# A new instruction order for attention, 480 slots per expert, and a third expert's weights loaded before the experts begin

## The chip, the cores and the metric

The kernel runs on one core of one Trainium2 chip. The metric is the device time of one launch in microseconds (us); lower is better.

## The reference

Attention with normalized queries and keys is followed by a mixture of experts in which a hash of the token's number chooses the one expert that a token goes to. All tensors are float32 and the token ids int64.

```python
batch, n_heads, seq, head_dim = (8, 12, 448, 64)
N, D, E, F = (3584, 768, 8, 1024)

def rmsnorm(x, g):
    rms = np.sqrt(np.mean(x * x, axis=-1, keepdims=True) + 1e-06)
    return x / rms * g
q_n, k_n = (rmsnorm(q, g_q), rmsnorm(k, g_k))
scores = scale * np.matmul(q_n, k_n.transpose(0, 1, 3, 2))     # scale = 1 / sqrt(64)
attn = softmax(scores)                                          # max taken off, sum + 1e-9
attn_out = np.matmul(attn, v)

x = attn_out.transpose(0, 2, 1, 3).reshape(B * S, H * D)        # one row per token
expert_idx = token_ids * 2654435761 % E
for e in range(E):
    mask = expert_idx == e
    h = np.maximum(x[mask] @ w1[e], 0.0)                        # w1[e]: 768 x 1024
    out[mask] = h @ w2[e]                                       # w2[e]: 1024 x 768
```

The inputs are the same draw each time.

## The kernel before

**Attention.** An image (one entry of the batch) has 12 heads, worked on as 6 pairs. One pair is one step, so there are 48 steps. Steps are put together in groups whose normalization is prepared at once: image 0 is cut into groups of 1, 2 and 3 pairs, every other image into two groups of 3, which makes 17 groups. The raw q, k and v of two images share one buffer each, and there are two buffers of each kind; GpSimd's queue loads them, with a cast to float16 or bfloat16. The pair 0 of image 0 comes in float32 through SyncE's and ScalarE's queues.

A group is prepared by squares of q and k (`prep_sq`, L275 on VectorE or L273 on ScalarE), sums of squares over the head dimension by matmuls with the identity (`prep_sum`, L287), their last reduction (`prep_red`, L298), logarithm and exponential on ScalarE for the inverse root (`prep_rr`, L306 and L307), the products (`prep_norm`, L319), and a copy of v beside a column of ones (`prep_v`, L330).

A step transposes its normalized q and k on PE (L477) into one PSUM bank of the pool `ps_qk`, which has one buffer and also takes the sums of squares. VectorE copies the bank out as kT and qT (L487, L489). Four pieces of scores (`score`, L498 and L503) go to three buffers of `ps_sc`; ScalarE takes their exponentials (L500, L505). `av_part` (L522 to L534) multiplies them with v in three parts; the ones give the row sums. VectorE then takes the reciprocal (L542) and the product (L543). When the 6 pairs of an image are done, its rows are stored to a scratch tensor in memory (`store_x`).

The order is written out by hand: every engine executes its instructions in program order, and within a step the program emits pieces 1 and 2 of the scores, the next step's transposes, piece 3, the former step's AV parts, the next step's piece 0 and what the lists `pre`, `mid` and `post` say is due. From step 14 on each step also emits one of 26 side jobs (`p1` to `p11`, `table`, `table_mm`) that turn token ids into slots and a table of row numbers per slot, `gidx`.

**Slots.** Each expert has CAP = 512 slots, 4 tiles of 128. The first three tiles of an expert hold only tokens of images 0 to 6, so that they can be gathered before image 7 is stored. Tokens that don't fit go to overflow blocks, worked through in a loop at the end with a count `n_ov` that is computed on the chip.

**Experts.** GpSimd gathers rows of the scratch tensor by `gidx` (L173), PE transposes them (`put_xT`, L184), `gemm1` multiplies with w1 over up to 512 columns of slots (L766), ScalarE and VectorE apply the maximum with zero (L770, L772), `gemm2` multiplies each tile of slots with w2 (L779), the result is copied out (L783) and scattered to the output rows (L784). Weights lie in four buffers: `w_pool` has two (experts 0, 1, 4, 5) and `w_pool2` two (experts 2, 3, 6, 7). Those of experts 0 and 1 are loaded during attention (L156, L162), those of 2 to 7 during the expert stage in six pieces each (`w_pieces`, `w_next`, L830), with expert e + 4's asked for when expert e is done. `fetch(e + 2)` asks for gathers two experts ahead. `turn(e + 1, kt)` transposes one tile of the next expert ahead of each tile of GEMM 2. The gathers of expert 0's first three tiles are emitted at step 44, and their transposes (to `xT_e`) after the last score piece.

All loads of q, k, v and weights, the gathers and the scatters are issued by GpSimd in its program order. Each of them waits until the transfer eight before it has landed, because eight semaphores are used in turn.

Of the kernel before, what the change touches and what calls it, by code (L numbers as in the profile page):

```python
# [19 lines left out]
def kernel(  # L20
# [28 lines left out]
    CAP = 512  # L49
    KT = CAP // P  # L50
# [26 lines left out]
    xg_e = [m_xe.tile([P, DIN], FP16, name=f"xg_{t}") for t in range(KT - 1)]  # L77
    xT_e = m_xe.tile([P, CO, CAP], FP16, name="xT_e")

# [24 lines left out]
    def setup():  # L104
        import dataclasses as _dc
        tid_t32 = _dc.replace(moe_token_ids.tensor, shape=[N * 2], dtype=I32)
        for base in (0, D):
            nc.sync.dma_start(out=gcol[base:base + D, 0:1], in_=g_q[:, None])
            nc.sync.dma_start(out=gcol[base:base + D, 1:2], in_=g_k[:, None])
        nc.scalar.dma_start(out=tid32[:],  # L110
                            in_=bass.AP(tensor=tid_t32, offset=0,
                                        ap=[[2 * NTC, P], [2, NTC], [1, 2]]))
# [36 lines left out]
    def load_w1(e, pool, dyn=None):  # L149
        w1_sb = pool.tile([P, CO, F], FP16, name="w1_sb")  # L150
# [8 lines left out]
    def load_w2(e, pool, dyn=None):  # L159
        w2_sb = pool.tile([P, FO, DIN], FP16, name="w2_sb")  # L160
# [4 lines left out]
    def load_w(e, pool):  # L165
        w_tiles[e] = (load_w1(e, pool), load_w2(e, pool))
# [32 lines left out]
    with tc.manual_schedule(), \  # L199
# [15 lines left out]
        q_bufs = [a_nat.tile([P, 2 * HP, 8, D], FP16, name=f"qr_{t}") for t in range(NB)]  # L215
        k_bufs = [a_nat.tile([P, 2 * HP, 8, D], FP16, name=f"kr_{t}") for t in range(NB)]
# [49 lines left out]
        def prep_sq(gi, a, on_act=False):  # L266
# [5 lines left out]
            if on_act:  # L272
# [4 lines left out]
        def prep_sum(gi, a, wide=False):  # L277
# [3 lines left out]
            if wide:  # L281
                T = ps_sc.tile([P, 2, 512], FP32, name="sc_ps")[:, 0]
            else:
                T = ps_qk.tile([P, 512], FP32, name="qkT_ps")
# [14 lines left out]


        def prep_rr(gi):
            n = groups[gi][2]
            ss = st[gi].pop("ss")
            m = 8 * n
            rr = a_st.tile([P, 2, GMAX * 8, 2], FP16, name="rr")
            nc.scalar.activation(ss[:, :, 0:m], ss[:, :, 0:m], AF.Ln, bias=eps_col[:], scale=1.0 / D)  # L306
# [3 lines left out]
            st[gi]["n8"] = a_n8.tile([P, 2, GMAX, 4, 2, D], FP16, name="n8")  # L310

        def prep_norm(gi):
            n = groups[gi][2]
            rr = st[gi].pop("rr")
            n8 = st[gi]["n8"]
            for a in (1, 0):
                f = raw(a, gi).rearrange("p n (hh j) (u t) -> p n hh j u t", hh=2, t=2)
                for hh in range(2):
                    nc.vector.tensor_tensor(  # L319
                        out=n8[:, a, 0:n, :, hh, :].rearrange("p n j (u t) -> p n j u t", t=2),  # L320
                        in0=f[:, :, hh],
                        in1=rr[:, a, 4 * n * hh:4 * n * hh + 4 * n].rearrange(
                            "p (n j) t -> p n j t", j=4)[:, :, :, None, :].to_broadcast(
                                [P, n, 4, D // 2, 2]),
                        op=ALU.mult)
# [63 lines left out]
        def p4():  # L389
# [6 lines left out]
            V.tensor_scalar(out=t1[:], in0=hole[:], scalar1=float(P - 1 - CAP), scalar2=0.0,  # L396
# [5 lines left out]
        def p5():  # L402
# [4 lines left out]
                            scalar2=float(E * CAP - CAP), op0=ALU.mult, op1=ALU.add)  # L407
# [13 lines left out]
        def p7():  # L421
            V.scalar_tensor_tensor(out=over[:], in0=rank[:], scalar=float(CAP), in1=bc(add_e[:]),
# [42 lines left out]
        qkt = {}  # L465
        pend = {}
        xs = {}

        def transposes(s, evac=True):
            gi, i = steps[s]  # L470
            n8 = st[gi]["n8"]
            T32 = ps_qk.tile([P, 512], FP32, name="qkT_ps")
            T = T32[:].bitcast(FP16)
            for a in (1, 0):
                for j in range(4):
                    o = 512 * a + P * j
                    nc.tensor.transpose(T[:, o:o + P], n8[:, a, i, j].rearrange("p h d -> p (h d)"),  # L477
                                        ident16[:])
            qkt[s] = T
            if evac:  # L480
                transposed(s)

        def transposed(s):
            T = qkt[s]
            kT = a_qk.tile([P, 512], FP16, name="kT")
            qT = a_qk.tile([P, S], FP16, name="qT")
            nc.vector.tensor_scalar(out=kT[:], in0=T[:, 512:1024], scalar1=g_col[:], scalar2=None,  # L487
                                    op0=ALU.mult)
            nc.vector.tensor_copy(qT[:], T[:, 0:S])  # L489
            qkt[s] = (qT, kT)  # L490

        def score(s, j):
            qT, kT = qkt[s]
            expT = pend[s][0]
            sc = ps_sc.tile([P, 2, 512], FP32, name="sc_ps")
            if j < 3:
                for hh in range(2):
                    nc.tensor.matmul(sc[:, hh, :S], lhsT=kT[64 * hh:64 * hh + 64, P * j:P * j + P],  # L498
                                     rhs=qT[64 * hh:64 * hh + 64, :], start=True, stop=True)
                nc.scalar.activation(expT[:, 2 * j:2 * j + 2, :], sc[:, :, :S], AF.Exp,  # L500
                                     bias=0.0, scale=1.0)
            else:
                nc.tensor.matmul(sc[:, 0, :S], lhsT=kT[:, 384:512], rhs=qT[:, :],  # L503
                                 start=True, stop=True)
                nc.scalar.activation(expT[:, 6, :], sc[:, 0, :S], AF.Exp, bias=0.0, scale=1.0)  # L505
                qkt.pop(s)
# [421 lines left out]
```

## Time and profile before

| | us |
|---|---|
| Median of 3 runs (lowest, highest) | 379.61 (378.47, 381.21) |
| The profiled execution | 374.72 |
| Span of that execution, first to last instruction | 373.2 |
| PE busy, share of the span | 343.4, 92% |
| VectorE (DVE) busy | 216.1, 58% |
| ScalarE (ACT) busy | 190.3, 51% |
| GpSimd (POOL) busy | 175.6, 47% |

The profile is of one execution. In its lines L12 is line 12 of the kernel, PEld is the weight load of a matmul, a form such as 128x512 is partitions by elements, and xN counts instructions. A timeline line has the start, the duration, the engine and its line, the operation with output<-input, and in brackets the idle time before it and what ended that. A line of windows has the stretch, its length, then for PE, PEld, DVE, ACT and POOL the busy time and in parentheses the number of instructions, then the granted PE clock as a share of full speed, a measure of DMA use and the GB/s moved. An average over the span says little here, since attention and experts have different limits; the stages have to be read one by one.

### The profile page before, as it was taken

To read this page: it belongs to the slowest core of one execution; us is meant where nothing else is said; L and a number is where in the kernel's file an instruction comes from. 1 tells how busy PE (TensorE), PEld (TensorE's weight loads), DVE (VectorE), ACT (ScalarE), POOL (GpSimd) and SP (SyncE) were. 2 spreads that over 40 slices of the span, in tenths; PEclk is the share of its full clock that TensorE was granted. 3 is DMA by queue.
4 is the path that set the end of the run, shared out by engine and by line. 5 is a ranking of instruction groups with operands and counts; after the bars stand their busy time and mean duration, and the time that the engine had idled before them with its cause. 6 is when DMAs were issued, how large, how long until landed. Compare 5 with 4: busy or idle time off the path is not lost. (4 is left out here: it accounts for less than half of the span.)

```text
span 373.2 us, 9220 instructions
## 1 busy us (share of the span) xinstructions
PE 343.4 (92%) x3862; PEld 231.1 (62%) x3862; DVE 216.1 (58%) x514; ACT 190.3 (51%) x288; POOL 175.6 (47%) x247
## 2 busy tenths in 40 slices
PE   7778879999989999999899999999998997999992
PEld 3456656767666666675676766666665664666661
DVE  4578979999999999989443333232232232332311
ACT  4777879999989999999312121211111111111110
POOL 8887981027439930003328335463654645633122
PEclk9999999999999999999899999999999999999997
DMA  8999999927999992274536999999999999972112
GB/s 123 159 192 195 185 221 191 216 40 127 194 211 211 223 217 52 46 162 108 128 93 141 209 238 252 211 261 223 203 254 177 250 219 188 241 259 91 58 42 112
DMA packets 54268, 64.59 MB, mean 173 GB/s; under 512 B 22403, under 2 KB 42134, under 8 KB 53968
## 3 DMA queue, kind: packets, MB, share of 16 engines
q0 software_dynamic: 50592, 57.98, 88.4%
q1 hardware_dynamic: 3024, 5.41, 5.3%
q8 instruction: 31, 0.51, 0.6%
q10 hardware_dynamic: 608, 0.59, 0.5%
q14 instruction: 13, 0.11, 0.1%
HBM read 89.68 MB, written 18.09 MB: 289 GB/s over the span
## 5 line engine op out<-in xcount | busy, mean ns | idle before, releaser
L500 ACT ACTIVATE expT<-sc_ps 128x896 bf16<-128x896 f32 x144 | 125.2, 923 | 10.8 <-PE sc_ps L498 9.8
L779 PE MATMUL o_ps<-w_sb,h_sb 128*128 128x256 f16 (+1 forms) x512 | 87.9, 326 | 0.0
L766 PEld LDWEIGHTS <-w_sb 128*128 128x128 f16 x432 | 58.0, 144 | 26.4 <-issue 2.0
L766 PE MATMUL h_ps<-xT,w_sb 128*128 128x512 f16 x336 | 73.7, 379 | 0.0
L779 PEld LDWEIGHTS <-h_sb 128*128 128x128 f16 x512 | 48.8, 98 | 32.7
L770 ACT ACTIVATE h_sb<-h_ps 128x512 f16<-128x512 f32 (+2 forms) x36 | 19.7, 549 | 77.2 <-PE h_ps L766 77.2
L784 POOL DMA_INDIRECT out_dram<-o_sb,gidx x32 | 32.9, 1029 | 49.0 <-ACT o_sb L783 17.0
L772 DVE TENSOR_SCALAR h_sb<-h_ps 128x512 f16<-128x512 f32 (+2 forms) x36 | 22.8, 632 | 56.3 <-PE h_ps L766 56.3
L173 POOL DMA_INDIRECT xg<-x_scratch,gidx x32 | 32.5, 1016 | 43.1 <-DVE xg L846 16.0
L783 ACT COPY o_sb<-o_ps 128x768 f32<-128x768 f32 x16 | 12.8, 798 | 74.8 <-PE o_ps L779 56.4
L498 PE MATMUL sc_ps<-qT,kT 64*128 64x448 f16 x288 | 44.0, 356 | 3.7 <-DVE qT L489 2.1
L522 PEld LDWEIGHTS <-expT 128*128 128x128 bf16 x864 | 37.0, 98 | 9.8 <-DVE x_sb L543 6.3
L522 PE MATMUL av_ps<-v,expT 128*128 128x65 bf16 x864 | 40.6, 194 | 1.5 <-DVE x_sb L543 1.5
L783 DVE COPY o_sb<-o_ps 128x768 f32<-128x768 f32 x16 | 15.3, 958 | 43.1 <-PE o_ps L779 21.2
L830 POOL DMA_DIRECT2D w_sb<-in_moe_w_dram x36 | 23.1, 648 | 31.2 <-DMA w_sb<-in_moe_w_dram 29.8
L477 PEld LDWEIGHTS <-n 128*128 128x128 f16 x384 | 22.4, 97 | 24.7 <-issue 15.4
L477 PE MATMUL qkT_ps<-ident,n 128*128 128x128 f16 x384 | 30.3, 220 | 6.7 <-DVE ss L298 3.8
L543 DVE TENSOR_TENSOR x_sb<-av_ps,srec 128x448 f16<-128x448 f32 x48 | 29.7, 619 | 1.5
L185 DVE COPY xT<-xT_ps 128x768 f16<-128x768 f16 x28 | 15.5, 554 | 25.3 <-PE xT_ps L184 25.2
L287 PEld LDWEIGHTS <-ident 128*128 128x128 f16 x544 | 23.6, 98 | 9.1 <-issue 6.5
L505 ACT ACTIVATE expT<-sc_ps 128x448 bf16<-128x448 f32 x48 | 26.9, 560 | 1.1 <-PE sc_ps L503 1.1
L487 DVE TENSOR_SCALAR kT<-qkT_ps,g_col 128x512 f16<-128x512 f16 x48 | 23.0, 480 | 4.1 <-PE qkT_ps L477 3.4
(145 smaller groups left out, 422.6 us busy)
## 6 DMA issues: line engine op xcount, KB each, us to landing
w_sb<-in_moe_w_dram POOLq DMA_DIRECT2D x32, 384.0 KB, 13.1
w_sb<-in_moe_w_dram POOLq DMA_DIRECT2D x12, 768.0 KB, 14.1
x_scratch<-x_sb SPq DMA_DIRECT2D x15, 288.0 KB, 5.9
w_sb<-in_moe_w_dram POOLq DMA_DIRECT2D x2, 1536.0 KB, 14.5
kr<-in_k_dram POOLq DMA_DIRECT2D x6, 384.0 KB, 10.2
qr<-in_q_dram POOLq DMA_DIRECT2D x3, 768.0 KB, 14.5
vr<-in_v_dram POOLq DMA_DIRECT2D x6, 384.0 KB, 19.8
kr<-in_k_dram POOLq DMA_DIRECT2D x6, 288.0 KB, 10.0
```

The lines of the kernel that those rows point to most:

```text
L173: nc.gpsimd.indirect_dma_start(out=xg[:], out_offset=None, in_=x_dram[0:rows, :], in_offset=bass.IndirectOffsetOnAxis(ap=idx, axis=0), bou ...
L287: nc.tensor.matmul(sp.rearrange("p (hh n j) w -> p hh n (j w)", hh=2, j=4), lhsT=ident16[:], rhs=sq[:, c, 0:m].rearrange("p (n hh j) w -> ...
L477: nc.tensor.transpose(T[:, o:o + P], n8[:, a, i, j].rearrange("p h d -> p (h d)"), ident16[:])
L498: nc.tensor.matmul(sc[:, hh, :S], lhsT=kT[64 * hh:64 * hh + 64, P * j:P * j + P], rhs=qT[64 * hh:64 * hh + 64, :], start=True, stop=True)
L500: nc.scalar.activation(expT[:, 2 * j:2 * j + 2, :], sc[:, :, :S], AF.Exp, bias=0.0, scale=1.0)
L505: nc.scalar.activation(expT[:, 6, :], sc[:, 0, :S], AF.Exp, bias=0.0, scale=1.0)
L522: nc.tensor.matmul(av[:, 2 * t + hh, :], lhsT=expT[:, tl(hh, j), P * t:P * t + P], rhs=v8[:, i, 4 * hh + j, 0:D + 1], start=(hh == 0 and t ...
L543: nc.vector.tensor_tensor(out=x_sb[:, :, hp * D:hp * D + D], in0=av[:, :, :D], in1=srec[:, :, None].to_broadcast([P, SL, D]), op=ALU.mult)
L766: nc.tensor.matmul(h_ps[:, :c1 - c0], lhsT=w1v[:, co, fo, :], rhs=xT[:, co, c0:c1], start=(co == 0), stop=(co == CO - 1))
L779: nc.tensor.matmul(o_ps[:, d0:d1], lhsT=h_sb[:, fo, col * P:(col + 1) * P], rhs=w2_sb[:, fo, d0:d1], start=(fo == 0), stop=(fo == FO - 1))
L783: (nc.vector.tensor_copy if col % 2 else nc.scalar.copy)(o_sb[:], o_ps[:])
L784: scat = nc.gpsimd.indirect_dma_start(out=out[:, :], out_offset=bass.IndirectOffsetOnAxis(ap=idx, axis=0), in_=o_sb[:], in_offset=None, bo ...
```

## The change

Three things change.

1. Attention's order. The loops over steps with `pre`, `mid` and `post` are replaced by text lists of tokens. One list covers the opening (steps 0 to 8 and parts of 9), and one block, `steady`, is emitted for each group from 4 on. A token is one operation: `sqq`, `sumk`, `redq`, `nk:1.0` and so on for a group, `Tk`, `kT`, `sc`, `exp`, `av`, `rec`, `x` for a step; numbers are relative to the group or step. For this `prep_norm`, `transposes`, `transposed`, `score` and the end of `av_part` are split into smaller pieces. Squares run on ScalarE for k of group 0 and k of group 3 (before: k and q of group 1, k of group 2).
2. A new prologue. The first loads bring q ahead of k; images 0 and 1 are loaded by half images and 2 to 7 one image at a time, each as q, k, v (before: images 2 and 3, 4 and 5, 6 and 7 together, first all k, then q, then v). GpSimd clears the second buffers before it loads image 2. The gains come in two transfers instead of four.
3. Experts use FIT = 480 of 512 slots, so the last tile of each has 96 (`LAST`). The weights of expert 2 go to the buffers that held raw q and k of images 0, 1, 4 and 5 (`qk_keep`, `w_views`) and their loads are emitted at steps 41 and 42; expert 6 uses the same buffers later. `w_pool2` has one buffer instead of two.

The core of the diff:

```diff
+    FIT = 480
+    LAST = FIT - 3 * P
...
+    qk_keep = [m_xe.tile([P, 2 * HP, 8, D], FP16, name=f"{a}r_0") for a in "qk"]
...
+    def w_views():
+        q0, k0 = [t[:].rearrange("p n s d -> p (n s d)") for t in qk_keep]
+        return (q0.rearrange("p (c f) -> p c f", f=F), k0.rearrange("p (f d) -> p f d", d=DIN))
...
+        ACT_SQ = ((0, 1), (3, 1))
+        WIDE_SUM = ((0, 0), (1, 0), (1, 1))
...
+        load_q([nc.sync, nc.scalar], first[:, 0], 0, 0, 1)
+        load_kv([nc.sync, nc.scalar, nc.sync, nc.scalar], first[:, 1], k, 0, 0, 1)
+        setup()
         nc.vector.memset(warm[:], 0.0)
...
+        load(0, 1, 2, "q")
+        make_identity(nc, ident16[:])
+        load(0, 1, 2, "k")
+        load(0, 0, 3, "v")
+        load(0, 3, 3)
+        load(1, 0, 3)
+        load(1, 3, 3)
         zero_kv(nc.gpsimd, k_bufs[1], 0, 2 * HP)
         zero_q(nc.gpsimd, q_bufs[1], 0, 2 * HP)
         zero_kv(nc.gpsimd, v_bufs[1], 0, 2 * HP)
+        load(2, 0, HP)
+        load(3, 0, HP)
+        for xg in xg_e:
+            nc.gpsimd.memset(xg[:], 0.0)
         setup2()
...
+        def hooks(s):
...
+            if s == HP:
+                load(4, 0, HP)
+            if hp == 3 and 1 <= b and b + 4 < B:
+                load(b + 4, 0, HP)
             if side and s >= 14:
                 side.pop(0)()
...
             if s == NS - 4:
                 for kt in range(KT - 1):
                     gather(xg_e[kt], gidx[:, kt:kt + 1], N_EARLY)
             if hp == 3:
...
                 if b == 6:
+                    w_tiles[1].append(load_w2(1, new_w2(w_pool)))
+            if b == 6 and hp == 5:
+                w_tiles[2] = w_views()
+                load_w1(2, w_tiles[2][0])
+            if b == 7 and hp == 0:
+                load_w2(2, w_tiles[2][1])
...
+        emit("""
+            zero:2 zero:0 zero:4 zero:1 sqq:0 zero:3 spin:9 sumq:0 sqk:0 sumk:0 spin:3 redq:0
+            sqq:1 redk:0 gain:0 ln:0 er:0 sumq:1 spin:1 redq:1 nk:0.0 sqk:1 nk:0.1 sumk:1 spin:1
+            nq:0.0 zero:5 nq:0.1 redk:1 ln:1 Tk:0 Tq:0 kT:0 qT:0 sc:0.0 er:1 sc:0.1 nk:1.0 nk:1.1
+            sc:0.2 nq:1.1 nq:1.0 exp:0.0 Tk:1 kT:1 exp:0.1 Tq:1 v:0 exp:0.2 qT:1 sc:1.0 exp:1.0
+            Tk:2 sc:0.3 sqk:2 Tq:2 av:0.0 kT:2 exp:0.3 qT:2 sc:1.1 sqq:2 sc:1.2 sc:1.3 sumk:2
...
+        """, 0, 0)
+        steady = """
+            Tk:1 Tq:1 sc:0.1 sc:0.2 av:-1.0 kT:1 av:-1.1 qT:1 exp:0.1 exp:0.2 v:1 sc:0.3 sumq:1
+            sqk:2 redq:1 av:-1.2 sc:1.0 sc:1.1 exp:0.3 ln:1 sc:1.2 er:1 Tk:2 exp:1.0 Tq:2 rec:-1
+            x:-1 av:0.0 nk:1.0 kT:2 qT:2 av:0.1 exp:1.1 sc:1.3 av:0.2 sumk:2 sc:2.0 exp:1.2
+            nk:1.1 sc:2.1 exp:1.3 nq:1.0 sc:2.2 exp:2.0 rec:0 nq:1.1 redk:2 Tk:3 x:0 Tq:3 av:1.0
+            kT:3 exp:2.1 av:1.1 qT:3 sqq:2 sc:2.3 av:1.2 rec:1 sc:3.0 exp:2.2 exp:2.3 x:1 exp:3.0
+        """
+        for g in range(4, NG):
+            emit(steady, g, s0[g])
...
-         tc.tile_pool(name="w_pool2", bufs=2) as w_pool2, \
+         tc.tile_pool(name="w_pool2", bufs=1) as w_pool2, \
...
         def gemm2(w2_sb, h_sb, col, idx, free=True):
+            w = LAST if free and col == KT - 1 else P
...
         fetch(1, range(KT - 1))
-        queue += w_pieces(2)
-        w_next(1)
         fetch(0, [KT - 1])
         fetch(1, [KT - 1])
         fetch(2, range(KT))
-        w_next(len(queue))
         queue += w_pieces(3)
...
-                gemm1(w1_sb, xTs.pop(e), h_sb, 0, CAP)
+                gemm1(w1_sb, xTs.pop(e), h_sb, 0, FIT)
...
-                    gemm1(w1_sb, xTs.pop(0), h_sb, EARLY, CAP)
+                    gemm1(w1_sb, xTs.pop(0), h_sb, EARLY, FIT)
```

The thresholds in `p4`, `p5` and `p7` that decide which tokens overflow use FIT in place of CAP; the distance between experts in the slot numbers stays 512. The hooks (loads, side jobs, gathers) of step s are emitted after the product `x` of step s - 1.

## Prediction

> **What bounds the kernel now.** I read the page's slices first, then busy time by stage, then the timelines of PE, DVE and POOL at the three places that the change touches. The chain of waits is no help: it ends after one step at the last scatter.
>
> ```profile
> PE   7778879999989999999899999999998997999992
> ...
> DVE  4578979999999999989443333232232232332311
> ACT  4777879999989999999312121211111111111110
> ...
> DMA  8999999927999992274536999999999999972112
> ```
>
> A slice is 9.3 us. There are two kernels in one: attention up to slice 19 (about 180 us), where DVE, ACT and PE are all near 9, and the experts, where PE alone is full. DMA has holes late in attention (slices 15 to 20) and is full during the experts.
>
> ```profile
> 50.00:55.00 5.00, 4.05 (x74) 2.81 (x73) 2.64 (x7) 3.78 (x5) 4.13 (x6) 1.00 1.37 236
> ...
> 80.00:100.00 20.00, 19.43 (x343) 13.79 (x342) 19.62 (x51) 18.95 (x29) 11.76 (x21) 1.00 0.87 125
> 100.00:120.00 20.00, 18.33 (x323) 12.86 (x319) 19.37 (x52) 18.40 (x29) 12.26 (x18) 1.00 1.50 209
> 120.00:140.00 20.00, 18.92 (x331) 13.20 (x328) 19.80 (x55) 18.64 (x29) 13.75 (x20) 1.00 1.03 219
> ```
>
> In these windows the third engine column is DVE and the fourth ACT. Between 60 and 160 us DVE is busy 97.7 of 100 us: it sets the pace of steady attention, whatever the order. The first 60 us are different: DVE 44.4 us, so 15.6 idle, 2.4 of them in the first row shown.
>
> ```profile
> 156.52 0.63 POOL L162 DMA_DIRECT2D w_sb<-in_moe_w_dram  x1 [22.75 <-PE sc_ps L498]
> 172.79 1.14 POOL L173 DMA_INDIRECT xg<-x_scratch,gidx  x1 [15.65 <-DVE xg L846]
> ...
> 178.47 0.50 PE L184 MATMUL qkT_ps<-ident,xg 128*128 128x128 f16 x6
> ...
> 185.90 2.98 PE L766 MATMUL h_ps<-xT_e,w_sb 128*128 128x384 f16 x17
> ```
>
> The hand-over: POOL issues w2 of expert 1 once the slot table's matmuls are through, and the gathers of expert 0 when image 6 is stored; PE transposes those rows at 178.47 and runs the bulk of the first GEMM from 185.90.
>
> ```profile
> 209.20 10.52 PE L766 MATMUL h_ps<-xT,w_sb 128*128 128x512 f16 x48
> 219.56 0.50 PE L184 MATMUL xT_ps<-ident,xg 128*128 128x128 f16 x6
> ...
> 286.97 0.51 PE L184 MATMUL xT_ps<-ident,xg 128*128 128x128 f16 x6 [0.95 <-DMA xg<-x_scratch,gidx]
> ...
> 296.37 0.50 PE L184 MATMUL xT_ps<-ident,xg 128*128 128x128 f16 x6 [0.41 <-DVE xT L185]
> ...
> 311.71 0.51 PE L184 MATMUL xT_ps<-ident,xg 128*128 128x128 f16 x6 [1.89 <-DMA xg<-x_scratch,gidx]
> ```
>
> In the experts PE is gapless but for these 3.25 us: gathers that landed late.
>
> **The Trainium skill.** "TensorE: Matmul & The Clock Gate", section "Wait — 56ns, not 53.3ns?", puts back-to-back matmuls at N columns over 2.4 GHz plus 2.5 ns. The trace agrees: 48 of 512 columns start over 10.36 us, 215.8 ns each. The same page, "What's actually happening", says that after a mostly idle window of about 3.4 us PE runs at half clock until it was busy as long; here PE is busy 0.35 to 0.76 of each us from 177 to 181, and 181 to 184 shows clocks of 0.54 and 0.50. "DMA: Bandwidth & Descriptors", section "Queues, rings and completion order": each DMA engine takes the descriptors of one queue in order and takes turns between queues. POOL's transfers indeed land in the order of issue throughout this trace, gathers and scatters behind weights, while SP's stores squeeze in between.
>
> **The change, part by part.** The sum is against the profiled execution, 374.72 us with a span of 373.2; the runs shown have a median of 379.61, 4.9 more. I carry the difference over.
>
> *480 slots.* The largest expert needs 465 slots (counted from the given token ids, holes for early slots included), so no overflow block arises. Seven experts x 48 matmuls go from 512 to 480 columns: 336 x 13.3 ns = 4.5 us. Expert 0's late slice goes from 128 to 96 columns; its 48 took 2.89 us, 60.2 ns each; by the page's rule 96 columns take 42.5, by no gain 60.2; I take 13.3 ns less, 0.6 us. GEMM 2 of the last tile streams the same 768 columns of w2, so its 96 slots save nothing on PE. Evacuations get shorter beside PE. Sum 5.1 (4.5 to 5.4).
>
> *Third expert early, as seen from the experts.* POOL's first gather per expert is issued at 223.94, 247.43, 270.57, 295.04, 318.72: 23.7 us apart, while PE needs 22.1 per expert (209.20, 231.30, 253.40, 275.50). DMA is slower than PE there, and PE lives on a lead until 286. Taking out five pieces of expert 2's weights (issued from 200.28, landed 206.2 to 219.4, so about 15 us of queue) gives that back. PE will need 21.5 per expert, so DMA then loses about 2.5 per expert over four experts, 10 us, less than 15. The 3.25 us go. If the lead does not hold, they stay. Experts in all: 5.1 + 3.25 = 8.4 saved (5.1 to 8.7).
>
> *Third expert early, as seen from the hand-over.* POOL does not follow the steps; it stops only at real waits. Right after w2(1) it can issue w1(2) and w2(2), since their buffers (raw q and k of images 4 and 5) were last read before 150. In coordinates of before: w2(1) issued 156.5, landed 167.5 (10.96 us). w1 pieces land 1.86 apart (118.74, 120.66, 122.52, 124.37), four 7.4; a whole w2 behind others took 7.7 (124.37 to 132.03); image 6's stores in between about 1.5 (in a like case a piece needed 3.3 instead of 1.86). So w2(2) lands at 184.1, and expert 0's gathers, behind it on one queue, at 185, 186 and 187, where before they landed at 176.0, 177.3 and 179.7. PE wants the first at 178.5: what waits behind is everything on PE, the last two AV parts and with them image 7's stores. Transposes end about 187.5 instead of 181.3. In the new PE order two of three AV(46) parts are ahead of them, so what follows is 0.3 + 1.0 (six GEMM matmuls) + 1.2 (AV 47) and half clock, 1.75 lost, as before had too: 42 GEMM matmuls start at an equivalent 191.8 against 185.9. Cost 5.9 us. From below: if the queue ran 3 us faster, 2.5; from above, with w2 at the 4.65 us per half that the experts' stage shows, 8.5. I take 5.9.
>
> *Prologue.* Squares of group 0 now run on DVE and ACT side by side (before one after the other on DVE, 0.69 and 0.68), and q comes first. Walked with the trace's durations: sq q 4.5, sums and ss to 7.0, rr 7.65; sq of k of group 1 waits for its keys (issue about 3 to 5 behind q and the identity, some 4 us to land) until 9.0; norms to 10.7; kT and qT to 11.9; first exp 12.3 against 13.69. Then transfers gate: keys of group 2 land about 16.4 (DVE ready at 14.4), of group 4 about 28.4 (27.3). Half-image loads need 40 POOL issues of about 0.65 us, until 27.6, then the zeroing of the second buffers (4.7 us, before behind all loads) comes ahead of image 2, whose keys land near 41.5; DVE is ready about 39. DVE work of the opening list after the first square: evacuations 7.2, row sums and x 6.3, squares 7.3, norms 8.9, v 2.2, sums and gain 2.6: 34.5. With these waits the list ends at about 50.5, having done 39 us of DVE work. Before reached 36.8 at 50 and then lost 2.4 on late values of image 2, which now come with their image. DVE has 0.9 more to do in all (three squares come from ACT, two go; zeros of v). Of 160.1 us, 121.1 remain, at the old share of 0.969 (114.8 of the 118.5 us from 60 to 178.5) until about 175.5 against 178.5; I add 1 us for steady blocks nearer full. Lead 4 us (0 to 9: from no gain, to 15.6 idle with half removed and no key late).
>
> *Steady blocks.* Same instructions, DVE-bound at 9.4 to 10 us per three steps; at most 2.3 us were idle. From 160 ACT is full instead (2.81 us a step), and nothing changes there.
>
> *Nothing:* tokens' load moved to SP (used at 72), gains in two transfers (needed about 7), later POOL constants (needed near 70), reciprocal split from the product. Hidden by the distance; if POOL's constants were late, side work would slip, not steps.
>
> Sum: -4.0 + 5.9 - 8.4 = -6.5. Profiled 368.2, median 379.6 - 6.5 = 373.1.
>
> **Rivals.** *Both covers hold (B):* image 2's keys are in time (lead 9) and the gathers cost only 2.5: -9 + 2.5 - 8.4 = -14.9, 364.7. For it: 15.6 us idle in the opening. Against: DMA is already at 9 in slices 1 to 7. *Order is worth nothing (C):* DVE was the bound, the opening is bound by transfers: 0.5 lead, -0.5 + 5.9 - 8.4 = -3.0, 376.6. For: DMA row; against: the chain to the first exp is plainly shorter. *Slower (D):* one PSUM bank serves all transposes and square sums, and the block of three steps interleaves sums with transposes; where DVE's reduction sits behind norms, PE waits for the bank, then DVE for PE. Before, PE waited up to 1.87 us at L477 on the reduction. A new wait of 0.8 us in each of 13 blocks adds 10.4: -4 + 10.4 + 5.9 - 8.4 = +3.9, 383.5; above 0.5 us per block it outweighs all gains. Against: each reduction stands well ahead of the next transposes in the list.
>
> **How the numbers follow.** Forecast 0.48, B 0.20, C 0.20, D 0.12. 1% (3.8 us) is about what a measurement of this kernel tells from no change. Faster by more: nearly all of the forecast (0.42), B, a little of C (0.04): 0.66. Within: 0.06 + 0.15 + 0.03: 0.24. Slower: 0.10. The range goes from B's time to a new wait of 0.55 us a block (-4 + 7.2 + 5.9 - 8.4 = +0.7): 364.7 to 380.3.
>
> **What would show it.** Right: GEMM 1 blocks of 9.7 us; no DMA wait at the experts' transposes; expert 0's gathers landing right after w2(2), PE idle 5 to 6 us before the first xT_e transposes, then half clock; first exp near 12.3; DVE stopped at image 2's key square near 39 to 42. Wrong: gathers landing before the weights, DVE under 95% between 60 and 160, or experts still waiting for gathers.

## The result, and the profile after

The changed kernel takes 391.75 us (median of 4 runs, 390.35 to 392.46) where the kernel before takes 379.04 on the same chip (4 runs): ratio 1.0325, 95% interval 1.0267 to 1.0383. It is slower by 12.7 us; 6.5 us faster was forecast. Chips differ: in later comparisons the kernel before had medians between 373.1 and 381.3 us, and a second comparison of the changed kernel gave 391.55 against 373.14, ratio 1.0489 (1.0407 to 1.0572). So I compare ratios, or kernels run on one chip. The profiled execution of the changed kernel took 390.35 us, with a span of 388.8, 15.6 more than the one before; that is more than the 12.7 of the medians, because the profiled execution before, with 374.72 us, was faster than the four runs measured beside the changed kernel (377.75 at the lowest).

First the slices of its page, 9.7 us each.

```profile
PE   6789699824999999989929999999999999999992
...
DVE  5689689642999999979713343333223333233310
ACT  3578689903999999979911112111211111121110
...
PEclk9589899955999999999957999999999999999999
DMA  8998998999699883229972399999999999912112
```

There is a hole that the kernel before has not: slices 8 and 9, counted from 0 (78 to 97 us), with ACT down to 0, DVE to 2 and PE's clock to half, while DMA stays at 9. The second weak place, slice 20, is the hand-over, the passage from attention to the experts. Next, the windows of the changed kernel from 60 us on, columns as before (PE, PEld, DVE, ACT, POOL); below them stands the window from 60 to 80 of the kernel before, whose windows from 80 to 140 the prediction shows.

```profile
60.00:80.00 20.00, 16.50 (x306) 12.08 (x305) 14.30 (x35) 17.88 (x28) 12.88 (x22) 0.99 1.21 171
80.00:100.00 20.00, 9.63 (x128) 6.80 (x130) 9.78 (x27) 6.15 (x9) 10.43 (x21) 0.58 1.39 177
100.00:120.00 20.00, 19.56 (x338) 13.46 (x335) 19.27 (x50) 18.91 (x29) 10.63 (x18) 1.00 1.15 171
120.00:140.00 20.00, 18.74 (x330) 13.01 (x328) 19.45 (x56) 18.55 (x29) 18.58 (x25) 1.00 0.87 178
140.00:160.00 20.00, 19.34 (x339) 13.58 (x337) 19.86 (x56) 19.12 (x31) 6.64 (x10) 1.00 0.51 100
```

```profile
60.00:80.00 20.00, 19.15 (x336) 13.62 (x335) 19.34 (x50) 19.12 (x30) 0.43 (x3) 1.00 1.33 169
```

From 100 to 160 DVE is busy 58.6 of 60 us: the steady block itself runs as forecast. From 60 to 100 DVE is busy 24.1 of 40 us, where the kernel before had 39.0. What ended its idle time stands in the timelines at that place: first POOL's, then lines of DVE, PE and ACT, and last the same two operations of the side jobs (POOL and DVE) in the kernel before.

```profile
70.49 0.75 POOL L239 DMA_DIRECT2D qr<-in_q_dram  x1 [0.92 <-DVE kT L496]
...
82.14 0.64 POOL L249 DMA_DIRECT2D vr<-in_v_dram  x1 [0.94 <-DMA qr<-in_q_dram]
82.78 0.22 POOL L377 CAST eidf<-eid 128x28 f32<-128x28 int32 x1
...
92.81 0.64 POOL L249 DMA_DIRECT2D vr<-in_v_dram  x1 [0.87 <-DMA qr<-in_q_dram]
93.45 0.20 POOL L384 CAST oc<-ot 128x8 bf16<-128x8 f32 x1
```

```profile
83.04 0.39 DVE L381 TENSOR_TENSOR onehot<-eidf,iota_f 128x224 bf16<-128x224 f32 x1 [7.85 <-POOL ones_e L378]
93.94 0.39 DVE L395 CAST cmix<-sc_ps 112x224 bf16<-112x224 f32 x1 [6.59 <-PE sc_ps L393]
93.71 0.17 PE L392 MATMUL sc_ps<-oc,emask 128*128 128x8 bf16 x1 [5.31 <-POOL oc L384]
87.05 2.54 ACT L525 ACTIVATE expT<-sc_ps 128x896 bf16<-128x896 f32 x3 [9.10 <-PE sc_ps L507]
```

```profile
72.19 0.21 POOL L367 CAST eidf<-eid 128x28 f32<-128x28 int32 x1 [13.17 <-DVE eid L365]
75.27 0.38 DVE L371 TENSOR_TENSOR onehot<-eidf,iota_f 128x224 bf16<-128x224 f32 x1
```

The conversion of the expert ids (side job p1, L377) takes 0.22 us on POOL, but POOL executes in order and has the ten transfers of image 5 in front of it, from 70.49 to 82.78. VectorE's next side operation (p2, L381) reads its result and waits 7.85 us, with all of VectorE's steady work queued behind it. In the kernel before GpSimd had nothing to do there: it waited 13.17 us for VectorE, converted at once, and VectorE's line has no bracket, so no wait. In the changed kernel the same happens again right away with p2's own conversion (L384), behind image 6: PE waits 5.31 us, VectorE for PE 6.59 us, ScalarE for scores 9.10 and 6.49 us. The transfers themselves were not urgent: image 5's first step is step 30, its keys are squared from step 24 on, and this is step 15. The last piece of exponential of step 16 comes at 77.4 us (76.7 before), that of step 19 at 102.9 (87.0 before).

The hand-over and the experts:

```profile
171.73 0.62 POOL L168 DMA_DIRECT2D w_sb<-in_moe_w_dram  x1 [25.08 <-PE sc_ps L462]
...
174.76 0.59 POOL L168 DMA_DIRECT2D kr<-in_moe_w_dram  x1
...
194.01 1.13 POOL L182 DMA_INDIRECT xg<-x_scratch,gidx  x1 [18.66 <-DVE xg L871]
...
200.71 0.82 PE L193 MATMUL qkT_ps<-ident,xg 128*128 128x128 f16 x6 [6.62 <-DMA xg<-x_scratch,gidx]
...
208.89 7.51 PE L788 MATMUL h_ps<-xT_e,w_sb 128*128 128x384 f16 x42
...
226.62 3.05 PE L788 MATMUL h_ps<-xT_e,w_sb 128*128 128x96 f16 x48 [0.65 <-DVE xT_e L194]
...
232.44 9.88 PE L788 MATMUL h_ps<-xT,w_sb 128*128 128x480 f16 x48
```

GpSimd issues w2 of expert 2 (into `kr`) at 174.76, and 19 us later the gathers, for which image 6 has to be stored first. PE waits 6.62 us for the gathered rows, then runs at half clock (an early transpose group takes 0.82 us instead of 0.50). A GEMM 1 block takes 9.88 instead of 10.52 us. To compare kernels I use three marks of the PE timeline: the 28 matmuls of the slot table (step 39), the bulk of expert 0's first GEMM, and the end of the span, in us:

| kernel | slot table | first GEMM | end | table to GEMM | GEMM to end |
|---|---|---|---|---|---|
| before | 155.09 | 185.90 | 373.2 | 30.8 | 187.3 |
| changed | 170.30 | 208.89 | 388.8 | 38.6 | 179.9 |
| changed, second comparison | 173.69 | 211.78 | 391.2 | 38.1 | 179.4 |
| changed, loads in pairs | 158.42 | 197.12 | 376.2 | 38.7 | 179.1 |
| changed, side jobs on VectorE | 157.03 | 195.74 | 375.2 | 38.7 | 179.5 |
| before, single loads | 159.16 | 188.47 | 375.9 | 29.3 | 187.4 |
| changed, gathers first | 172.23 | 202.97 | 390.2 | 30.7 | 187.2 |
| changed, weights ahead | 171.70 | 200.92 | 380.4 | 29.2 | 179.5 |
| before, experts' part | 157.08 | 196.38 | 375.7 | 39.3 | 179.3 |
| both moves | 158.93 | 188.15 | 367.2 | 29.2 | 179.1 |
| both moves, image 1 whole | 155.24 | 184.46 | 363.4 | 29.2 | 178.9 |
| both moves, more idle matmuls | 160.33 | 191.08 | 370.2 | 30.8 | 179.1 |
| both moves, image 1 whole, more idle matmuls | 154.99 | 184.21 | 363.1 | 29.2 | 178.9 |
| the same, later copy of values | 154.88 | 192.54 | 371.9 | 37.7 | 179.4 |
| before, experts' part, weights ahead | 157.18 | 195.09 | 374.9 | 37.9 | 179.8 |

The other kernels of the table are the experiments below. The 15.6 us are +15.2 up to the slot table, +7.8 at the hand-over and -7.4 in the experts.

### The profile page after: what moved, and what is told of

The parts are those of the page before. It is cut to its first block, busy times and chain, and to the rows that moved or that the text cites. A ratio compares the mean times of both kernels' runs of the same rounds, so it can differ in the third digit from the quotient of the medians.

```text
span 388.8 us, 9220 instructions
## 1 busy us (share of the span) xinstructions
PE 340.9 (88%) x3841; PEld 236.8 (61%) x3841; DVE 212.6 (55%) x515; ACT 186.3 (48%) x285; POOL 197.3 (51%) x286
## 5 line engine op out<-in xcount | busy, mean ns | idle before, releaser
L802 PEld LDWEIGHTS <-h_sb 128*128 128x128 f16 (+1 forms) x512 | 51.2, 104 | 30.5
L802 PE MATMUL o_ps<-w_sb,h_sb 128*128 128x512 f16 (+3 forms) x384 | 65.8, 326 | 0.0
L807 POOL DMA_INDIRECT out_dram<-o_sb,gidx x32 | 32.4, 1014 | 60.4 <-ACT o_sb L806 32.8
L792 ACT ACTIVATE h_sb<-h_ps 128x480 f16<-128x480 f32 (+2 forms) x36 | 18.8, 526 | 84.7 <-PE h_ps L788 81.0
L788 PEld LDWEIGHTS <-w_sb 128*128 128x128 f16 x336 | 44.3, 146 | 16.5 <-issue 2.0
L794 DVE TENSOR_SCALAR h_sb<-h_ps 128x480 f16<-128x480 f32 (+2 forms) x36 | 21.7, 602 | 54.8 <-PE h_ps L788 52.3
L788 PE MATMUL h_ps<-xT,w_sb 128*128 128x480 f16 x240 | 49.4, 366 | 0.0
L542 PE MATMUL av_ps<-v,expT 128*128 128x65 bf16 x864 | 42.5, 197 | 1.2 <-DVE x_sb L571 0.5
L299 PEld LDWEIGHTS <-ident 128*128 128x128 f16 x544 | 26.5, 103 | 22.8 <-DVE qT L499 17.4
L806 DVE COPY o_sb<-o_ps 128x768 f32<-128x768 f32 (+1 forms) x16 | 15.3, 956 | 39.6 <-PE o_ps L802 31.7
L528 ACT ACTIVATE expT<-sc_ps 128x448 bf16<-128x448 f32 x48 | 28.1, 585 | 10.7 <-PE sc_ps L510 10.7
L249 POOL DMA_DIRECT2D vr<-in_v_dram x40 | 25.6, 657 | 14.2 <-DMA qr<-in_q_dram 12.6
L299 PE MATMUL qkT_ps<-sq_k,ident 128*128 128x96 f16 (+1 forms) x256 | 15.0, 217 | 15.9 <-DVE qT L499 13.8
```

The lines of the kernel that those rows point to most:

```text
L299: nc.tensor.matmul(sp.rearrange("p (hh n j) w -> p hh n (j w)", hh=2, j=4), lhsT=ident16[:], rhs=sq[:, c, 0:m].rearrange("p (n hh j) w -> ...
L542: nc.tensor.matmul(av[:, 2 * t + hh, :], lhsT=expT[:, tl(hh, j), P * t:P * t + P], rhs=v8[:, i, 4 * hh + j, 0:D + 1], start=(hh == 0 and t ...
L788: nc.tensor.matmul(h_ps[:, :c1 - c0], lhsT=w1v[:, co, fo, :], rhs=xT[:, co, c0:c1], start=(co == 0), stop=(co == CO - 1))
L802: nc.tensor.matmul(o_ps[0:w, d0:d1], lhsT=h_sb[:, fo, col * P:col * P + w], rhs=w2_sb[:, fo, d0:d1], start=(fo == 0), stop=(fo == FO - 1))
L806: (nc.vector.tensor_copy if col % 2 else nc.scalar.copy)(o_sb[0:w], o_ps[0:w])
L807: scat = nc.gpsimd.indirect_dma_start(out=out[:, :], out_offset=bass.IndirectOffsetOnAxis(ap=idx[0:w], axis=0), in_=o_sb[0:w], in_offset=N ...
```

## The experiments

Theory 1: GpSimd's queue. Image loads stand ahead of small operations that others wait for. Its rival is theory 2, close to D of the prediction: the steady block's own order. The hand-over is a question of its own.

**Loads in pairs.**

```diff
-            if s == HP:
-                load(4, 0, HP)
-            if hp == 3 and 1 <= b and b + 4 < B:
-                load(b + 4, 0, HP)
+            if hp == 3 and b % 2 and b + 3 < B:
+                load(b + 3, 0, 2 * HP)
```

> The changed kernel, but with images 4 and 5 loaded together at step 9 and 6 and 7 together at step 21 (10 transfers for two images, as the kernel before has it), where it loads them one by one at steps 6, 9, 15 and 21. Theory 1 (GpSimd's queue: image loads stand ahead of the side jobs' small GpSimd operations, and VectorE, then PE and ScalarE, stop for these): 60 to 104 us gets back 13 to 16 us, the conversion of the expert ids runs near 72 instead of 82.8, VectorE is busy over 19 of 20 us in every stretch from 60 to 160, and the time is 375 to 379. Theory 2 (the order of the steady block itself, for example the one PSUM bank of transposes and square sums): the stretch from 60 to 104 stays slow and the time stays within 3 us of 391.7. Theory 3 (half as many transfers of twice the size bring images 4 to 7 too late): a new stop at an image's key square, and 383 or more.

378.46 us against 374.27: ratio 1.0144 (1.0066 to 1.0222). The slot table comes at 158.42, 11.9 us earlier than in the changed kernel. A closer comparison is "gathers first" below, which ran on the same chip and has the changed kernel's attention as it is: there the table comes at 172.23 and the kernel takes 391.3 us. A window of this kernel and a line of VectorE's timeline:

```profile
80.00:100.00 20.00, 19.11 (x337) 13.33 (x334) 18.82 (x52) 18.69 (x28) 10.29 (x19) 1.00 1.30 172
```

```profile
76.70 0.39 DVE L381 TENSOR_TENSOR onehot<-eidf,iota_f 128x224 bf16<-128x224 f32 x1 [1.49 <-POOL ones_e L378]
```

The stop at L381 shrinks from 7.85 to 1.49 us and DVE is busy 18.82 of 20 us where it had 9.78. No new stop at an image's keys appears, so the third theory of the expectation falls. The rest of the expectation was too clean: the conversion runs at 76.44, not near 72, because the pair of images 4 and 5 is in front of it, and from 60 to 80 DVE is busy only 17.58 us.

**Side jobs on VectorE.**

```diff
-            G.tensor_copy(eidf[:], eid[:])
-            G.memset(ones_e[:], 1.0)
+            V.tensor_copy(eidf[:], eid[:])
+            V.memset(ones_e[:], 1.0)
...
-            G.tensor_copy(oc[:], ot[:])
+            V.tensor_copy(oc[:], ot[:])
```

and so on in p4 and p5.

> The changed kernel with its loads where they are, but all GpSimd operations of side jobs p1, p2, p4 and p5 given to VectorE (15 small ones). Theory 1 (the wait is for GpSimd's turn, not for data): the three stops of VectorE of 7.9, 6.6 and about 3 us between 74 and 101 go, VectorE gets 2 to 3 us of work more, and the time is 377 to 381. Theory 2 (the steady block's order): within 3 us of 391.7, or slower by the work added to VectorE.

377.48 us, 1.012 (1.006 to 1.018). Loads stay where they were and VectorE has more to do, yet the time comes back:

```profile
74.65 0.38 DVE L381 TENSOR_TENSOR onehot<-eidf,iota_f 128x224 bf16<-128x224 f32 x1
```

There is no bracket: no wait. Theory 1 is shown from two sides, by moving what was in the way and by moving what waited, both on the chip of "gathers first". Theory 2 falls as the cause of the loss. The slot table is still 1.9 to 3.3 us later than before (157.03 and 158.42 against 155.09); "image 1 whole" below brings it to 155.24.

**Single loads in the kernel before.** The opposite edit.

```diff
-            if hp == 1 and b % 2 and b + 3 < B:
-                load_qk(b + 3, 0, 2 * HP)
-                load_v(b + 3, 0, 2 * HP)
+            if s == HP:
+                load_qk(4, 0, HP)
+                load_v(4, 0, HP)
+            if hp == 3 and 1 <= b and b + 4 < B:
+                load_qk(b + 4, 0, HP)
+                load_v(b + 4, 0, HP)
```

> The kernel before with one thing of the change: images 4 to 7 are loaded one by one at steps 6, 9, 15 and 21. Theory 1: the load of image 6 now stands ahead of p2's conversion on GpSimd, so VectorE and PE stop in steps 15 to 18; there is no backlog on GpSimd here (its constants are done before), so only one load of about 10 us is in the way: 4 to 10 us slower, 383 to 389. If the backlog alone is what hurts: within 2 us of 379. Theory 2: within 2 us of 379.

377.26 us, 1.0113 (1.0032 to 1.0194): 3.0 us more than the median before on this chip, just under "4 to 10 us", with an interval too wide to tell it from "within 2 us". The stops are there but short (VectorE at L385 and L487, 1.49 and 1.26 us, both for PE), as GpSimd was done with its constants at 49.0 and only one load was in the way. So single loads alone do not cost 15 us. In the changed kernel they meet the backlog of the new prologue, where images 2 and 3 are issued until 52.5, the constants until 60.8, and image 4 until 69.6.

**Gathers first.** The loads of expert 2's weights leave steps 41 and 42.

```diff
                     gather(xg_e[kt], gidx[:, kt:kt + 1], N_EARLY)
+                w_tiles[2] = w_views()
+                load_w1(2, w_tiles[2][0])
+                load_w2(2, w_tiles[2][1])
```

> The changed kernel, but with the weights of expert 2 asked for right after expert 0's three gathers instead of ahead of them. If the hand-over loss is the queue ahead of the gathers (weights of 3 MB between the last store's data and them): PE's idle 6.6 us before the early transposes goes and the time is 383 to 386. If the gathers wait for the stores of image 6 alone (these landed 7 to 9.5 us after their issue because the weights share the DMA engines), they also land earlier, since the weights no longer run beside the stores: 382 to 385. If expert 2's weights are then late for expert 2: a stop of PE at expert 2, and no gain.

391.3 us, 1.0472 (1.0413 to 1.0531): no gain against the changed kernel, which took 391.75 and 391.55 us on two other chips. The hand-over is as short as before (30.7 us), but the wait has moved. PE's timeline:

```profile
216.47 0.80 PE L193 MATMUL xT_ps<-ident,xg 128*128 128x128 f16 x6 [6.43 <-DMA xg<-x_scratch,gidx]
```

Now expert 1's first gather is behind the 3 MB. My last line had the stop at expert 2, one expert too late. Placed at the hand-over, ahead of or behind the first gathers, these weights make PE wait 6.4 to 6.6 us.

**Weights ahead.**

```diff
-            if b == 6 and hp == 5:
+            if s == NS - 11:
                 w_tiles[2] = w_views()
                 load_w1(2, w_tiles[2][0])
-            if b == 7 and hp == 0:
+            if s == NS - 10:
                 load_w2(2, w_tiles[2][1])
```

> The changed kernel, but with the weights of expert 2 asked for at steps 37 and 38, ahead of w2 of expert 1 in GpSimd's queue, where it asks at 41 and 42, behind it. Image loads and side jobs stay as they are. GpSimd waits about 25 us for the slot table before w2 of expert 1, and the DMA engines move little in that time, so the 3 MB should land there. If the hand-over loss is these weights running beside image 6's stores and ahead of expert 0's gathers: the stores land 3 us after their issue, PE's 6.6 us before the early transposes go, and the time falls by 6 to 8 us against the changed kernel. If the weights' early transfer is not what delays the gathers: within 2 us of the changed kernel.

 

> The changed kernel as it is, to have it on the same chip as the next three. Expected: 1.03 times the kernel before, and 12 to 15 us more span than the variant with paired loads had.

381.91 us, 1.0236 (1.0154 to 1.0319), against 391.55 of the changed kernel on the same chip: 9.6 us gained, more than the 6 to 8 expected. The control behaved as expected but for the ratio, 1.049 instead of 1.03. The stores of image 6 take 3.3 us where they took 8.2 in the changed kernel, and PE's timeline has no wait for gathers at the hand-over and full clock:

```profile
195.32 0.50 PE L193 MATMUL qkT_ps<-ident,xg 128*128 128x128 f16 x6
...
200.92 3.15 PE L788 MATMUL h_ps<-xT_e,w_sb 128*128 128x384 f16 x18
```

**The experts' part alone, in the kernel before.** Attention's order and loads as before, and of the change:

```diff
+    FIT = 480
+    LAST = FIT - 3 * P
+    qk_keep = [m_xe.tile([P, 2 * HP, 8, D], FP16, name=f"{a}r_0") for a in "qk"]
...
+            if b == 6 and hp == 5:
+                w_tiles[2] = w_views()
+                load_w1(2, w_tiles[2][0])
+            if b == 7 and hp == 0:
+                load_w2(2, w_tiles[2][1])
...
-        queue += w_pieces(2)
-        w_next(1)
```

> The kernel before with the experts' part of the change alone: 480 slots, the weights of expert 2 in the raw buffers, asked for at steps 41 and 42; attention's order, prologue and image loads are those of before. By the prediction's steps: hand-over +5.9, experts -8.4, so 2.5 us faster than before; by the changed kernel's trace +7.8 and -8.0, so no difference. If the hand-over loss comes only with the new order: 8 us faster.

377.12 us, 1.0092 (1.0065 to 1.0119), so it is slower than before by a little. The experts gain 8.0 us (187.3 to 179.3), the hand-over gives back 8.5 (30.8 to 39.3); 2.0 more come ahead of the slot table, where the two kernels have the same instructions, and are not explained. Of the three expectations "no difference" is nearest, and the new order is not needed for the hand-over loss. The issues of 155 to 192 us in this kernel show the mechanism (KB of each, median us from issue to landing; the weights of expert 2 go into `qr` and `kr`), with GpSimd's issue of w2 and PE's wait below:

```profile
w_sb<-in_moe_w_dram POOLq DMA_DIRECT2D x1, 1536.0 KB, 10.9
qr<-in_moe_w_dram POOLq DMA_DIRECT2D x4, 384.0 KB, 16.0
kr<-in_moe_w_dram POOLq DMA_DIRECT2D x1, 1536.0 KB, 25.8
x_scratch<-x_sb SPq DMA_DIRECT2D x2, 288.0 KB, 8.1
```

```profile
161.53 0.61 POOL L167 DMA_DIRECT2D kr<-in_moe_w_dram  x1
...
187.89 0.82 PE L192 MATMUL qkT_ps<-ident,xg 128*128 128x128 f16 x6 [7.29 <-DMA xg<-x_scratch,gidx]
```

w2 of expert 2 was issued at 161.53, so it landed at 187.3; PE gets the first gathered rows at 187.89. SP's stores of image 6, in another queue, took 8.1 us beside these weights, and 3.3 in "weights ahead", where the weights have gone by. The Trainium skill, "DMA: Bandwidth & Descriptors", section "Issuing engines are not separate DMA queues", says that transfers of all issuing engines interleave on the same 16 DMA engines, and this trace agrees. The gathers' issue waits for these stores, too: the first gather is issued 12.0 us after the first store here and 6.3 us after it in the kernel before.

**Both moves.** Loads in pairs and weights ahead together.

> The changed kernel with both moves: images 4 and 5, 6 and 7 loaded in pairs at steps 9 and 21, and the weights of expert 2 asked for at steps 37 and 38. If the two losses are apart (GpSimd's queue in attention, the weights ahead of the gathers), they add: 1.0144 times before less 6 to 8 us, so 4 us faster than before, ratio 0.985 to 0.995. If the first only hides the second: ratio over 1.0.

369.31 us, 0.9909 (0.9879 to 0.994), as expected. The two losses are separate and add up: loads in pairs alone gave some 13 us, weights ahead alone 9.6, and both together 22.2 (391.55 to 369.31, on one chip).

**Image 1 whole.** On top of both moves.

```diff
-        load(1, 0, 3)
-        load(1, 3, 3)
+        load(1, 0, HP)
```

> The variant with both moves, and image 1 loaded whole (10 transfers) where the changed kernel loads it in two halves (20). In the opening GpSimd issues a transfer each 0.6 us, and 10 fewer leave it 6 us earlier at the zeroing and at image 2. If GpSimd's issuing is what makes image 2's keys late: VectorE's stop of 3.4 us at their square and PE's and ScalarE's after it go, the ids' conversion is no longer behind the loads of images 4 and 5 either (76.9 before, near 72 now), and the time falls by 4 to 7 us against the variant with both moves, to 0.973 to 0.982 of the kernel before. If the DMA engines are the limit there (the prediction's reason): image 2 comes no earlier, within 1.5 us of the variant with both moves.

364.14 us, 0.9735 (0.968 to 0.979), faster than both kernels. GpSimd starts image 2 at 28.1 instead of 33.3 (32.4 in the changed kernel) and VectorE's stop at its keys is gone. This is the stop as the changed kernel had it:

```profile
44.42 0.96 DVE L287 TENSOR_TENSOR sq_k<-kr 128x1536 f16<-128x1536 f16 x1 [3.64 <-DMA kr<-in_k_dram]
```

So GpSimd's issuing of many small transfers was the limit there. In the kernel with image 1 whole, VectorE's timeline shows what is late next, and from 60 to 80 VectorE is busy 19.02 us, where the changed kernel had 14.30:

```profile
30.06 0.56 DVE L340 COPY v<-vr 128x1536 bf16<-128x1536 bf16 x1 [4.26 <-DMA vr<-in_v_dram]
```

```profile
60.00:80.00 20.00, 19.13 (x342) 13.78 (x340) 19.02 (x50) 19.55 (x31) 6.98 (x13) 1.00 1.48 206
```

**More idle matmuls.** On top of both moves, then on top of image 1 whole.

```diff
-            zero:2 zero:0 zero:4 zero:1 sqq:0 zero:3 spin:9 sumq:0 sqk:0 sumk:0 spin:3 redq:0
-            sqq:1 redk:0 gain:0 ln:0 er:0 sumq:1 spin:1 redq:1 nk:0.0 sqk:1 nk:0.1 sumk:1 spin:1
+            zero:2 zero:0 zero:4 zero:1 sqq:0 zero:3 spin:12 sumq:0 sqk:0 spin:6 sumk:0 spin:5 redq:0
+            sqq:1 redk:0 gain:0 ln:0 er:0 sumq:1 spin:4 redq:1 nk:0.0 sqk:1 nk:0.1 sumk:1 spin:4
```

> The variant with both moves, with more idle matmuls in the opening (12, 6, 5, 4 and 4 instead of 9, none, 3, 1 and 1), so that PE has no idle stretch up to 11 us. If half clock from 8 to 21 us is what held the first exponential at 14.3: the clock stays over 0.9 from 5 us on, the first exponential comes 1 to 2 us earlier; but VectorE's stop at image 2's keys then takes it back, and the time is within 1.5 us of the variant with both moves. If not, more matmuls only delay the opening: later by up to 1 us.

 

> Both moves, image 1 whole and the added idle matmuls. Now that image 2's keys do not hold the opening, the earlier first exponential stays: 1 to 2 us faster than the variant with image 1 whole alone, 0.968 to 0.978 of the kernel before. If the opening is bound by GpSimd's transfers still: equal to it.

370.27 us, 0.9894 (0.9831 to 0.9957), and 364.83 us, 0.9766 (0.9725 to 0.9807): neither differs from its base. The window of 10 to 15 us in both moves without, then with them, and last in image 1 whole without them:

```profile
10.00:15.00 5.00, 3.64 (x33) 2.32 (x33) 3.77 (x11) 1.91 (x5) 3.86 (x8) 0.50 1.29 155
```

```profile
10.00:15.00 5.00, 3.14 (x40) 1.92 (x38) 4.22 (x13) 2.62 (x6) 4.88 (x9) 1.00 1.37 168
```

```profile
10.00:15.00 5.00, 2.74 (x36) 1.63 (x35) 4.64 (x14) 2.48 (x6) 4.73 (x9) 1.00 1.32 162
```

The clock is back at 1.00, but the first exponential comes at 13.84 instead of 14.19, 0.35 us and not 1 to 2. From 5 to 25 us VectorE then does 15.0 us of work instead of 13.1, but it stops 2.94 us for image 1's keys at 30.74 and 2.25 us for image 2's at 44.35, and the slot table is no earlier. Half clock was not what held the opening. The third window shows that image 1 whole, in its trace, had full clock without any added matmuls, so there the added ones had nothing to restore. It also raises a rival: the gain of image 1 whole might be that of the clock. The two kernels with added matmuls answer it. Both have full clock, both ran on one chip, and they differ in image 1 whole alone: 370.27 against 364.83 us.

**Later copy of values, and the old order.** One token moves, on top of all the others; and, on the same chip, the kernel before with the experts' part and weights ahead (the edit of "weights ahead" on "the experts' part alone").

```diff
-            sc:3.0 v:3 sc:3.1 exp:3.0 sc:3.2 av:2.0 exp:3.1 sumk:3 av:2.1 sqq:3 redk:3 sc:3.3
+            sc:3.0 sc:3.1 exp:3.0 sc:3.2 av:2.0 exp:3.1 sumk:3 av:2.1 sqq:3 redk:3 sc:3.3
...
-            er:3 Tq:5 nk:3.0 kT:5 exp:4.0 av:3.0 exp:4.1 qT:5 av:3.1 nq:3.0 nq:3.1 exp:4.2 sc:4.3
+            er:3 Tq:5 nk:3.0 kT:5 exp:4.0 v:3 av:3.0 exp:4.1 qT:5 av:3.1 nq:3.0 nq:3.1 exp:4.2 sc:4.3
```

> The variant with both moves, image 1 whole and the added idle matmuls, and one token moved: the copy of image 1's values, which stopped VectorE for 4.3 us at 25.8 us once image 1 came whole, stands just ahead of their first use, some 30 tokens later. If that stop alone is left in the opening: 3 to 4 us faster, 0.965 to 0.970 of the kernel before. If another transfer is late next (image 2's keys near 40): within 1.5 us of 0.976.

 

> The kernel before with its own attention order, prologue and image loads, and the experts' part of the change with the weights of expert 2 asked for at steps 37 and 38. This weighs the new order of attention. By the traces so far the slot table's matmuls come at 155.1 us in the kernel before and at 155.2 in the best variants of the new order, so the new order gains nothing by then; the hand-over is 29 to 31 us and the experts save 8: 364 to 367, 0.972 to 0.980 of the kernel before, the same as the new order with its loads mended. If the new order is worth something after step 39: 0.980 or more.

The first: 371.35 us against 381.3, 0.9732 (0.9669 to 0.9795), no gain that can be told from 0.9766. In its trace PE, VectorE and ScalarE stand still for over 4 us up to 181, for a releaser that the profile calls remote, and the hand-over takes 37.7 us. So only the kind of wait in the opening is read from it:

```profile
29.27 1.48 ACT L285 ACTIVATE sq_k<-kr 128x1536 f16<-128x1536 f16 x1 [3.71 <-DMA kr<-in_k_dram]
```

The copy of the values no longer stops VectorE; the keys of image 1 hold ScalarE's square instead, so the opening waits for transfers in turn. The second: 374.81 us, 0.9843 (0.9786 to 0.99), outside the 0.972 to 0.980 of the first expectation and within the second, that the new order is worth something after step 39. The new order, together with the new prologue and its mended loads, is 3.5 us faster on that chip than the old order and prologue. The traces don't show where. The slot table comes at 154.99 with all but the token's move and at 157.18 in the old order, and 155.09 in the unchanged kernel; from the first GEMM on the two differ by under 1 us. In the old order's trace PE, VectorE and ScalarE also stand still for about 3 us up to 183, again with "remote", PE then runs at half clock, and the hand-over takes 37.9 us, which hides what the order is worth there. I have no cause for these stops. What the order alone is worth stays open: the 3.5 us are what the runs show for order, prologue and image loads together.

## Why the prediction was wrong

**Attention's lead, -4.0: the step that failed.** It came out at +15.2 at the slot table. The steady blocks were put at no change, and the wrong sentence stands under "Nothing": "if POOL's constants were late, side work would slip, not steps". The constants were in time (done at 60.8, needed near 70), but they and the loads of the new prologue kept GpSimd busy until then, so that the loads of images 4 to 6 came to stand in front of the side jobs' conversions. And side work does not slip: its VectorE and PE operations stand in the same queues as the steps, in program order, so a side job that waits for GpSimd stops the steps behind it, 7.85 and then 6.59 us on VectorE. I had walked GpSimd's queue to image 2's keys and again from w2 of expert 1 on, but never from 41 to 94 us, where the changed hooks put images 4, 5 and 6 ahead of p1 and p2. The terms were at hand: images at about 10 us each, constants and zeroing of 8.4 us, loads at steps 6, 9 and 15, side jobs from step 14. Apart from that, the lead itself never came: with step 16's exponentials, as the first of the two stops begins, the changed kernel is 0.7 us later than before.

**The opening.** The stop of VectorE at image 2's keys came where it was put: VectorE is ready at 40.8 (put at about 39) and stops for 3.64 us, as the keys come at 44.4 (put at 41.5). The reason given in the walk, GpSimd's 40 issues and the zeroing ahead of image 2, was right, as image 1 whole showed; the walk had not asked what fewer issues would give. The first exponential was put at 12.3 and came at 14.27: PE waits 1.81 us for ScalarE's square of the first keys and then runs at half clock, and the walk had neither. Full clock brings back only 0.35 us of it, as the added idle matmuls showed; the rest is not settled.

**The hand-over, +5.9.** The mechanism was right, with gathers landing right behind w2 of expert 2, PE idle 6.62 us and then half clock. The size was 7.8 in the changed kernel, 8.5 in the experts' part alone, and undoing it gave back 8.9 on one chip (38.1 to 29.2). That is the upper end of the 2.5 to 8.5 given, or just above it. What I left out is what the weights do to the stores: these take about 8 us beside them, and so the gathers' issue comes later too.

**The experts, -8.4.** Measured -7.4, and -8.4 in the best variant. GEMM 1 gave 7 x 0.64 = 4.5 us as forecast, and no transposes wait for gathers any more. The late slice gave nothing of the 0.6 us: 48 matmuls of 96 columns take 3.05 us, as 48 of 128 columns did, 60.2 ns from start to start in both. The saving of 13.3 ns per matmul is there from 512 to 480 columns (215.8 to 202.5 ns) and not from 128 to 96: the page's rule that the prediction used, 42.5 ns for 96 columns, is not met by these short matmuls, and the measurement decides.

**The rivals.** D had the right sign for the wrong reason. It named a wait for a PSUM bank in each of 13 blocks, while the steady blocks run full from 100 us on and the loss is two long stops and what follows from them. Its 383.5 us was still 8 too low.

## What to carry to other kernels

Walk every in-order queue from end to end when loads on it move, and ask for each small operation what stands in front of it and who waits for it; here two conversions of 0.2 us behind prefetches that nobody needed yet cost some 12 us or more, where the experts gained 7.4. A prefetch is best placed where its queue and the DMA engines are idle and nothing urgent follows: here the same 3 MB cost about 8 us at the hand-over and nothing that the marks show four steps earlier. Splitting transfers to get the first part sooner costs the issuing engine time for all that is queued behind: image 1 in 20 transfers instead of 10 put image 2 off by 5.2 us.

## What the runs showed of the hardware that I had not expected

48 matmuls with 96 moving columns took as long as 48 with 128: 3.05 us, start of the first to end of the last, in both. Image loads of ten transfers each kept GpSimd occupied 8.7 to 12.3 us an image (60.87 to 69.57 and 70.49 to 82.78), although an issue itself takes about 0.65 us, 6.5 for ten; much of the rest is waits for an earlier transfer to land, as in the bracket of the line at 82.14. Half clock in the opening of both moves (0.50 from 10 to 20 us) put the first exponential off by only 0.35 us, and the 1.9 us of VectorE's work that it cost by 25 us were no gain when they came back, since VectorE then waited for keys.
